# Another order of the first loads, sums of absolutes on ACT for the first weights, and scratch rows of 1 KB, in a chunked-attention and mixture-of-experts kernel

## The chip, the cores and the metric

One core of a Trainium2 chip runs the whole program in one launch. The engines are PE (matrix products and transposes), ACT (activations, copies with a scale), DVE (elementwise work and reductions), POOL (elementwise work, slower) and SP, which here only issues DMAs. The metric is the device time of the program in us; less is better.

## The reference

Attention in chunks of 32 tokens, each with 16 tokens of context to its left, 8 to its right and 8 memory tokens; then eight experts on all tokens, their outputs weighted by a matrix P that eight rounds of row and column scaling make out of gate logits.

```python
def _attn_ref(q, k, v, mem_k, mem_v):      # q, k, v: (4, 8, 768, 64), mem: (4, 8, 8, 64)
    for c in range(nc):                    # 24 chunks of 32
        k_full = np.concatenate([mem_k, k[:, :, l_start:r_end]], axis=2)
        v_full = np.concatenate([mem_v, v[:, :, l_start:r_end]], axis=2)
        scores = scale * np.matmul(q_c, k_full.transpose(0, 1, 3, 2))
        a = np.exp(scores - np.max(scores, axis=-1, keepdims=True))
        a = a / (np.sum(a, axis=-1, keepdims=True) + 1e-09)
        out[:, :, c_start:c_end] = np.matmul(a, v_full)

def _moe_ref(x, w_gate, w1, w2):           # x: (3072, 512), w1: (8, 512, 1024), w2: (8, 1024, 512)
    logits = x @ w_gate
    P = np.exp(logits - logits.max())
    for _ in range(8):
        P /= P.sum(1, keepdims=True) + 1e-09
        P /= P.sum(0, keepdims=True) + 1e-09
        P *= N / E
    for e in range(E):
        out += P[:, e:e + 1] * (np.maximum(x @ w1[e], 0.0) @ w2[e])
```

## The kernel before

**Work.** The 3072 tokens are 24 blocks of 128 for the attention (6 per batch) and 6 units of 512 for the experts, so four blocks feed one unit. There are 48 pairs of expert and unit. Products of the experts run in float16, each operand split in a high and a low half (`split`: ACT writes the high half, DVE the rest), three matmuls for one; and by Strassen's scheme of seven products instead of eight (`px`, `py`, `pz` for x times w1, `yx`, `yy`, `yz` for h times w2). Expert 0 in its first unit goes without that scheme (`pp` for x times w1, `yp` for h times w2), since it needs less preparation. The first of these `pp` products is called the first product below.

**Scales.** Before a matrix is split it is scaled by a power of two. For weights, `most` takes the largest absolute value of each partition of a staged tile on DVE (`mxs`), `scales` reduces over the four tiles (`most_of`), PE transposes that column (`row_w`), DVE reduces it, and PE spreads the result to all partitions (`sp_w`); the scale `sw` follows. For the tokens, the values v give the bound (`vmax`, `row_x`, `sp_x`, `sx`).

**Attention of a block.** q and k are loaded by SP (`load_block`), a few rows of the neighbour and the memory keys as `kx` (`load_extra`), values as windows of 56 rows (`load_values`, tiles `v_pair`, `w_0_2`, `w_0_3`, `x_room`). PE transposes q, k and kx (`tq`, `tk`, `tx`), ACT copies them (`qT`, `kC`, `kxT`), PE makes scores (`sp`), DVE the softmax's maximum and difference, ACT the exponential (`s`), PE transposes (`ta`), ACT copies (`at`), PE multiplies by the values (`xp`), DVE divides (`xq`), PE transposes (`xt`) and ACT copies into `xg`, the unit's tokens.

**Order.** A planner (`Plan`) holds all tasks with a cost, an engine and a due time, runs them through in a model of its own, and so writes the order of every engine once, when the program is built; on the chip each engine works through its row in order and waits on semaphores. DMAs have a cost in that model too (`dma=`, `ISSUE`, `BEHIND`, `FIRST`). Where the model sees a gap on PE of over 0.4 us, `pad` fills it with matmuls on the identity that nobody reads (`warm`), so that PE stays busy. Their number is fixed in the program.

**Scratch.** Tokens in their split form are kept in DRAM (`xkeep`, 1.8 MB a unit) and loaded again for each expert; the sums of the outputs (`akeep`) and some tokens (`gkeep`) as well. A tile of w1 is two loads of 256 KB with rows of 512 bytes.

Of the kernel before, what the change touches and what calls it, by code (L numbers as in the profile page):

```python
# [11 lines left out]
F16 = mybir.dt.float16  # L12
# [9 lines left out]
SHIFT = 11  # L22
HSHIFT = 18
ISSUE = 0.5
BEHIND = 5.0
FIRST = 2.0
MARGIN = 8.0
APART = 3.6
# [3 lines left out]
class Task:  # L32


    __slots__ = ("eng", "cost", "fn", "prio", "left", "ready", "end", "then", "takes", "frees", "n", "dma", "start", "many")
# [55 lines left out]
class Plan:  # L91
# [14 lines left out]
    def add(self, eng, cost, fn, deps=(), prio=0.0, bufs=(), takes=None, frees=None, dma=0.0, many=False):  # L106
# [3 lines left out]
        t.many = many  # L110
        if dma:
            t.cost = cost * ISSUE
# [51 lines left out]
    def run(self):  # L164
        clock = {e: 0.0 for e in self.ENGINES}
        waiting = {e: [] for e in self.ENGINES}
        able = {e: [] for e in self.ENGINES}
        dma = FIRST
# [4 lines left out]
        while left:  # L173
# [45 lines left out]
            for s in t.then:  # L219
                s.left -= 1  # L220
                late = lag
                if s.eng == t.eng and not t.dma:
                    late = 0.0
                elif t.dma and self.fill is not None:

                    late = MARGIN if s.prio - t.end > FAR else 0.0
# [7 lines left out]
def tile_chunked_attn_sinkhorn_moe(  # L234
# [83 lines left out]
    ones = one.broadcast_to([P, P])  # L318
    idle = ident.bitcast(BF16)
# [114 lines left out]
    def scales(part, s, u, name, deps, prio, pool=None):  # L434
# [20 lines left out]
        def inverse(a):  # L455
            nc.vector.tensor_scalar_mul(u, a, 2.0**-SHIFT)
# [74 lines left out]
    w1v = w1.rearrange("e (kt p) (fh fp f) -> e fp p kt fh f", p=P, fh=2, fp=FP)  # L531
    w2v = w2.rearrange("e (fh fp p) d -> e fp p fh d", fh=2, fp=FP)
# [3 lines left out]
    def load(e, fp, which, prio, ahead="", eng="SP", after=()):  # L536
        shape = [P, 2, KT, P] if which == 1 else [P, 2, DM]
# [8 lines left out]
        def go():  # L546
            if which == 1:
                for fh in range(2):
                    queue.dma_start(st.t[:, fh], w1v[e, fp, :, :, fh])
# [3 lines left out]
        return st, add(eng, 2 if which == 1 else 1, go, after, prio, [st], dma=2.1)  # L553

    def most(e, fp, which, st, deps, prio):
        def go():
            flat = st.t.rearrange("p a k f -> p (a k f)" if which == 1 else "p a d -> p (a d)")
# [10 lines left out]
    def scale_w(e, which, deps, prio, pool=None):  # L568
# [9 lines left out]
            pool,  # L578
        )
# [14 lines left out]
    def cut(e, fp, which, st, ld, prio):  # L594
# [12 lines left out]
        if which == 1:  # L607
            a11, a12 = lambda: st.t[:, 0, 0:2], lambda: st.t[:, 0, 2:4]
            a21, a22 = lambda: st.t[:, 1, 0:2], lambda: st.t[:, 1, 2:4]
# [25 lines left out]
        if which == 1:  # L635
# [3 lines left out]
                    lambda: st.t[:, 0],  # L639
# [21 lines left out]
        else:  # L661
            pieces = [(slice(2, 3), slice(0, 1), (0.5, 0.65)), (slice(4, 7), slice(1, 4), (0.9, 1.1))]
            deps = deps + o.users
        for to, of, costs in pieces:
            done.append(
                split(
                    lambda j, to=to: o.t[:, j, to].rearrange(flat),
                    lambda of=of: ws.t[:, of].rearrange(flat),
# [19 lines left out]
    def plain1(fp, st, ld, prio):  # L688

        o = operands("w1", [P, 2, 7, 2, P], f"w1_0_{fp}")  # L690
        done = split(
            lambda j: o.t[:, j, 0:4].rearrange("p o k f -> p (o k f)"),
            lambda: st.t.rearrange("p a k f -> p (a k f)"),
# [9 lines left out]
    def block1(e, i):  # L703
        return i if e > 0 else (0, 1, 3, 2, 4, 5, 6)[i]
# [22 lines left out]
    vfound = []  # L727
    sxs = {}
# [3 lines left out]
    BLOCKS = (-50.0, -44.0, -30.0, -26.0)  # L732
# [30 lines left out]
    def load_extra(u):  # L763
# [10 lines left out]
        for n in range(n0, n0 + BU):  # L774
# [5 lines left out]
            def go(b=b, blk=blk, r0=r0, t0=t0):  # L780
# [5 lines left out]
                elif blk == NB - 1:  # L786
                    nc.sync.dma_start(kx.t[r0 : r0 + LC], rows(k, b, S - LC, LC))
                    nc.sync.dma_start(kx.t[r0 + LC : r0 + KR], rows(k, b, 0, KR - LC))
                else:
# [5 lines left out]
                    2 if blk in (0, NB - 1) else 1,  # L795
# [1532 lines left out]
```

## Time and profile before

| what | value |
|---|---|
| median of 3 runs | 1921.61 us (1919.76 to 1923.17) |
| the profiled execution | 1919.81 us |
| its span, first to last instruction | 1917.9 us |
| PE busy | 1903.2 us, 99% |
| DVE busy | 1436.4 us, 75% |
| ACT busy | 1033.6 us, 54% |
| granted clock of PE | 1.00 |

The page is of one execution. A row of a timeline gives start, length, engine, line, operation, the tile written and those read, how many, and in brackets the idle time before it with what ended it. A row of the waits gives the engine and line that waited, what for, the sum in us, the number and the longest. PEld is the load of weights into PE, which runs beside PE.

### The profile page before, as it was taken

What the parts mean: (1) busy time and instruction counts of PE and PEld (TensorE: products, weight loads), DVE (VectorE), ACT (ScalarE), POOL (GpSimd) and SP (SyncE); (2) the same over time, 40 slices, a digit from 0 to 9 for tenths busy, and PEclk for the clock granted to TensorE, in tenths of its full rate; (3) what the DMA queues carried; (4) which work ended last, traced back from release to release, by engine and by line L of the source; (5) the groups of instructions that cost most, each with busy time, mean ns of one, the idle gap of its engine ahead of it and who ended that gap; (6) DMA issues with size and microseconds to landing.
All of it is one profiled execution on the core that took longest, in us unless ns stands there. A gap on an engine that the chain in (4) does not pass through costs nothing.

```text
span 1917.9 us, 47295 instructions
## 1 busy us (share of the span) xinstructions
PE 1903.2 (99%) x19616; PEld 1641.0 (86%) x19616; DVE 1436.4 (75%) x2396; ACT 1033.6 (54%) x2019; POOL 524.4 (27%) x549
## 2 busy tenths in 40 slices
PE   9999999999999999999999999999999999999999
PEld 7777676688888888888888888888888888888888
DVE  6776569778679866898668875898678885786565
ACT  4765565556456545646445554655555554564453
POOL 1220001544224221432124231342124232332112
PEclk9999999999999999999999999999999999999999
DMA  8678753453235342265214533245313732322321
GB/s 198 174 194 209 171 172 116 129 204 125 83 110 172 127 148 85 78 197 185 92 63 149 197 105 127 78 160 176 138 45 105 242 122 94 100 83 84 127 83 67
DMA packets 246791, 254.82 MB, mean 133 GB/s; under 512 B 113264, under 2 KB 180272, under 8 KB 242224
## 3 DMA queue, kind: packets, MB, share of 16 engines
q1 hardware_dynamic: 244452, 251.21, 41.2%
q8 instruction: 153, 2.51, 0.6%
q10 hardware_dynamic: 2124, 0.59, 0.2%
q14 instruction: 62, 0.51, 0.1%
HBM read 187.84 MB, written 63.44 MB: 131 GB/s over the span
## 4 chain that ended last, share of the span: by engine, by line
PE 96%; DMA 2%; DVE 1%; ACT 0%; issue 0%; SPq 0%; ACTq 0%; DVEq 0%
PE px L1598 26%; PE yx L1598 23%; PE pz L1598 13%; PE yz L1598 11%; PE py L1598 6%; PE yp L2126 6%; PE yy L1598 6%; DMA q<-in_q_dram 1%; PE xp L1137 1%; PE sp L1069 1%; PE pp L2045 1%; PE tq L1006 1%; PE tk L1010 0%; PE ta L1127 0%; PE xt L1178 0%; DVE w L521 0%
## 5 line engine op out<-in xcount | busy, mean ns | idle before, releaser
L1598 PEld LDWEIGHTS <-w 128*128 128x128 f16 x7896 | 771.4, 98 | 91.9 <-issue 0.6
L1598 PEld LDWEIGHTS <-h 128*128 128x128 f16 x7056 | 690.4, 98 | 81.4 <-issue 1.5
L1598 PE MATMUL px<-x,w 128*128 128x256 f16 x4512 | 549.1, 273 | 0.0
L1931 POOL TENSOR_TENSOR acc<-acc,y 128x256 f32<-128x256 f32 x252 | 267.5, 1068 | 862.1 <-ACT y L1906 842.7
L1598 PE MATMUL yx<-w,h 128*128 128x256 f16 x4032 | 467.5, 273 | 1.3 <-DVE acc L1941 1.3
L1657 ACT ACTIVATE q<-px 128x256 f32<-128x256 f32 x376 | 142.8, 381 | 294.2 <-PE px L1598 289.5
L1598 PE MATMUL pz<-x,w 128*128 128x256 f16 x2256 | 278.2, 273 | 0.0
L1598 PE MATMUL yz<-w,h 128*128 128x256 f16 x2016 | 233.8, 273 | 0.0
L1826 DVE TENSOR_TENSOR h<-ss,h 128x1024 f16<-128x1024 f32 x160 | 215.0, 1346 | 4.0 <-ACT h L1802 3.5
L1777 ACT ACTIVATE h<-c 128x768 f16<-128x768 f32 x168 | 140.8, 838 | 106.4 <-DVE c L1667 106.4
L1802 ACT CAST h<-ss 128x1024 f16<-128x1024 f32 x168 | 174.1, 1039 | 20.4 <-DVE ss L1766 19.6
L1766 DVE SCALAR_TENSOR_TENSOR ss<-c,ss 128x256 f32<-128x256 f32 x336 | 168.3, 501 | 8.2
L1810 DVE SCALAR_TENSOR_TENSOR h<-c,h 128x768 f16<-128x768 f32 x168 | 165.3, 984 | 9.2 <-ACT h L1777 9.1
L1667 DVE SCALAR_TENSOR_TENSOR c<-px,q 128x256 f32<-128x256 f32 x188 | 78.0, 422 | 103.2 <-PE px L1598 94.9
L1906 ACT ACTIVATE y<-yx,pscale 128x256 f32<-128x256 f32 x168 | 79.4, 473 | 114.8 <-PE yx L1598 110.6
L1598 PE MATMUL py<-x,w 128*128 128x256 f16 x1128 | 139.2, 273 | 0.0
L2126 PE MATMUL yp<-w,h 128*128 128x512 f16 x576 | 132.0, 379 | 0.0
L1667 DVE SCALAR_TENSOR_TENSOR c<-py,q 128x256 f32<-128x256 f32 x188 | 78.5, 422 | 60.2 <-PE py L1598 56.7
L1766 DVE SCALAR_TENSOR_TENSOR ss<-c,h 128x512 f32<-128x512 f32 x168 | 120.8, 719 | 3.1 <-ACT h L1754 3.0
L1598 PE MATMUL yy<-w,h 128*128 128x256 f16 x1008 | 116.9, 273 | 0.0
L2126 PEld LDWEIGHTS <-h 128*128 128x128 f16 x576 | 56.0, 98 | 57.9
L513 ACT ACTIVATE w<-ws,sw 128x1024 f16<-128x1024 f32 (+1 forms) x64 | 69.3, 1089 | 65.5 <-POOL ws L602 65.5
(158 smaller groups left out, 1773.0 us busy)
## 6 DMA issues: line engine op xcount, KB each, us to landing
x<-xkeep SPq DMA_DIRECT2D x28, 1792.0 KB
akeep<-acc SPq DMA_DIRECT2D x168, 256.0 KB
acc<-akeep SPq DMA_DIRECT2D x168, 256.0 KB
w1f<-in_moe_w_dram SPq DMA_DIRECT2D x72, 256.0 KB
w2f<-in_moe_w_dram SPq DMA_DIRECT2D x32, 512.0 KB
w1fm<-in_moe_w_dram SPq DMA_DIRECT2D x56, 256.0 KB
w2fm<-in_moe_w_dram SPq DMA_DIRECT2D x28, 512.0 KB
xkeep<-x SPq DMA_DIRECT2D x6, 1792.0 KB
```

Of the source, the lines that this page charges most:

```text
L513: lambda: nc.scalar.activation(dst(0), src(), AF.Copy, scale=s),
L1598: nc.tensor.matmul(dst.t, a, b, start=(not more and n == 0), stop=(n == end), skip_group_check=more,)
L1657: lambda: nc.scalar.activation(t.t, src.t, AF.Copy, scale=DOWN),
L1667: lambda: nc.vector.scalar_tensor_tensor(c.t[:, o], src.t, DOWN, q.t, op0=ALU.mult, op1=ALU.add),
L1766: lambda: nc.vector.scalar_tensor_tensor(dst(), src(), 0.0, other(), op0=ALU.max, op1=op),
L1777: lambda: nc.scalar.activation(h.t[:, 0, 0:3], c.t, AF.Relu),
L1802: lambda: nc.scalar.copy(h.t[:, 0, 3:7], ss.t),
L1810: lambda: nc.vector.scalar_tensor_tensor(h.t[:, 1, 0:3].rearrange("p a n -> p (a n)"), c.t.rearrange("p a n -> p (a n)"), 0.0, h.t[:, 0, 0 ...
L1826: lambda: spare.tensor_tensor(h.t[:, 1, 3:7], ss.t, h.t[:, 0, 3:7], op=ALU.subtract),
L1906: (lambda: nc.scalar.activation(t.t, src.t, AF.Copy, scale=f))
L1931: lambda: nc.gpsimd.tensor_tensor(acc.t[:, cols], acc.t[:, cols], q.t, op=ALU.add),
L2126: nc.tensor.matmul(py.t, hf.t[:, hl, where[fh], o : o + P], room(fp, WIDE * wl + DM * fh, WIDE * wl + DM * (fh + 1)), start=(fp == 0 and i ...
```

## The change

It has four parts. **First loads:** SP now issues q, k and kx of blocks 0 and 1 ahead of all values; the values of those two blocks come as 2 + 8 larger loads, all by SP, where SP and ACT shared them; some rows that only masked places see are not loaded any more (two small pieces of k and v per batch end), and zeros are written for block 0 by POOL. ACT does an exponential of one column at the start, which brings the table load to the front. **First weights:** a tile of w1 is one load with rows of 1 KB (the columns of the two halves are neighbours now, and the tiles are addressed accordingly), and the four w1 and four w2 tiles of expert 0 get their bound from a sum of absolutes on ACT (`total`) where DVE took maxima; their scale has a shift of 13 for 11. **Scratch:** `xkeep`, `gkeep` and `akeep` have rows of 1 KB in DRAM, where they had 14 KB, 4 KB and 2 KB. **Planner:** other constants, DMA costs and due times, and a model of eight loads in flight.

```diff
-ISSUE = 0.5
-BEHIND = 5.0
-FIRST = 2.0
+ISSUE = 0.45
+LANES = 8
+BEFORE = 0.7
+TABLE = 2.2
...
-APART = 3.6
+APART = 2.5
...
-                at = max(at, dma - BEHIND)
-                t.start = at
-                clock[t.eng] = at + t.cost
-                dma = max(dma, at + t.cost / 2) + t.dma
-                t.end = max(dma, at + t.cost) + 2.6
+                t.start = max(at, lanes[0])
+                for _ in range(t.count):
+                    at = max(at, lanes.pop(0))
+                    dma = max(dma, at + BEGIN) + t.dma / t.count
+                    lanes.append(dma + AFTER)
+                    at += ISSUE
+                clock[t.eng] = at
+                t.end = dma + AFTER
...
+    first = misc.tile([P, 1], F32, name="first")
+    nc.scalar.activation(first, one, AF.Exp)
...
-    xkeep = [dram.tile([P, 2 * 7 * 2 * GT], F16, name=f"xkeep_{u}") for u in range(NU)]
-    gkeep = [dram.tile([P, KT * GT], F32, name=f"gkeep_{g}") for g in range(2 * NU)]
-    akeep = [dram.tile([P, DM], F32, name=f"akeep_{T}") for T in range(NT)]
+    xkeep = [dram.tile([2 * 7, P, 2 * GT], F16, name=f"xkeep_{u}") for u in range(NU)]
+    gkeep = [dram.tile([KT, P, GT], F32, name=f"gkeep_{g}") for g in range(2 * NU)]
+    akeep = [dram.tile([2, P, DH], F32, name=f"akeep_{T}") for T in range(NT)]
...
-    w1v = w1.rearrange("e (kt p) (fh fp f) -> e fp p kt fh f", p=P, fh=2, fp=FP)
-    w2v = w2.rearrange("e (fh fp p) d -> e fp p fh d", fh=2, fp=FP)
+    w1v = w1.rearrange("e (kt p) (fp f) -> e fp p kt f", p=P, fp=FP)
+    w2v = w2.rearrange("e (fp fh p) d -> e fp p fh d", fh=2, fp=FP)
...
-                for fh in range(2):
-                    queue.dma_start(st.t[:, fh], w1v[e, fp, :, :, fh])
+                queue.dma_start(st.t.rearrange("p k a f -> p k (a f)"), w1v[e, fp])
...
+    def total(e, fp, which, st, deps, prio):
+        def go():
+            nc.scalar.activation(
+                room(0, 0, 1024),
+                st.t.rearrange("p k a f -> p (k a f)" if which == 1 else "p a d -> p (a d)"),
+                AF.Abs,
+                accum_out=mxs[:, e, which - 1, fp : fp + 1],
+            )
+
+        return add("ACT", 1.2, go, deps, prio, [st, first2[0]])
...
-    BLOCKS = (-50.0, -44.0, -30.0, -26.0)
+    BLOCKS = (-50.0, -49.0, -30.0, -26.0)
...
+        if n == 0:
+            ks.append(add("POOL", 0.2, lambda: nc.gpsimd.memset(kt.t[0:LC], 0.0), (), at, [kt]))
...
+            if n == 0:
+                lv = [
+                    add("SP", 2 + 2 * HP, lambda: go_both(nc.sync), (), at, [vt], dma=4.2),
+                    add("POOL", 0.2, clear, (), at, [vt]),
+                ]
+            elif n == 1:
+                lv = list(vs[0][1])
...
-            at = START - 14.0 + n // 2 * 17.0
-            vfound.append(add("DVE", 1.21, most, lv, at, [vt]))
-            if n == BU // 2 - 1:
-                scale_x(NU, vmax[:, 0:2], vfound, START - 12.0)
+            at = (5.0, 12.0, 33.0, 33.0)[n]
...
-            found.append(most(0, fp, which, st, [ld], at - 12.0))
-        scale_w(0, which, found, at - 10.0, "att")
+            found.append(total(0, fp, which, st, [ld], at - 12.0))
+        scale_w(0, which, found, at - 10.0, "att", SHIFT + 2)
```

What the planner makes of it shows in the rows of the engines (line, operation, tile written, tiles read, shape). On SP, the issue of the first loads, before, up to the first weights (`w1f`); nine more loads of `v_pair` stood in ACT's row:

```order
L848 DMA q_165<-in_q_dram 128x8x64
L842 DMA k_167<-in_k_dram 16x8x64
L843 DMA k_167<-in_k_dram 112x8x64
L782 DMA kx_175<-in_k_dram 24x8x64
L783 DMA kx_175<-in_mem_k_dram 8x8x64
L790 DMA kx_175<-in_k_dram 32x8x64
L921 DMA v_pair<-in_v_dram 16x4x64
L921 DMA v_pair<-in_v_dram 40x4x64
L921 DMA v_pair<-in_v_dram 56x4x64 x3
L848 DMA q_188<-in_q_dram 128x8x64
L845 DMA k_192<-in_k_dram 128x8x64
L790 DMA kx_175<-in_k_dram 32x8x64 x2
```

On SP after the change, the same place:

```order
L880 DMA q_165<-in_q_dram 128x8x64
L875 DMA k_163<-in_k_dram 112x8x64
L816 DMA kx_172<-in_k_dram 24x8x64
L817 DMA kx_172<-in_mem_k_dram 8x8x64
L823 DMA kx_172<-in_k_dram 32x8x64
L880 DMA q_178<-in_q_dram 128x8x64
L877 DMA k_180<-in_k_dram 128x8x64
L823 DMA kx_172<-in_k_dram 32x8x64 x2
L959 DMA v_pair<-in_v_dram 40x4x64 x2
L967 DMA v_pair<-in_v_dram 56x7x64 x8
L943 DMA v_pair<-v_pair 8x7x260 x2
L560 DMA w1f_0_325<-in_moe_w_dram 128x4x256
```

The second block's q and k moved ahead of the values, and the weights follow the values as one load a tile. On DVE, before, from the maxima of the first weights to the first row that splits them (`w_0_0`):

```order
L558 TENSOR_REDUCE mxs<-w1f_3_376 128x1
L502 TENSOR_REDUCE most_of<-row_x_564 1x1
L450 TENSOR_SCALAR most_of<-most_of 1x1
L451 TENSOR_SCALAR most_of<-most_of 1x1
L445 TENSOR_REDUCE most_of<-mxs 128x1
L456 TENSOR_SCALAR ux<-sp_x_617 128x1
```

On ACT after the change, where the sums of the first weights stand (they write `mxs`; the tile `w_0_0` takes the absolutes, which nobody reads):

```order
L581 ACTIVATE w_0_0_434,mxs<-w1f_0_325 128x1024
L1171 ACTIVATE s_436<-s_436 128x512
L581 ACTIVATE w_0_0_434,mxs<-w1f_1_327 128x1024
L1247 COPY xg_476<-xt_465 128x4x128
L1209 COPY at_481<-ta_471 128x512
L581 ACTIVATE w_0_0_434,mxs<-w1f_2_330 128x1024
L581 ACTIVATE w_0_0_434,mxs<-w1f_3_332 128x1024
```

The four passes over the weights left DVE's row and stand in ACT's, between the copies of the attention. In DVE's row the reduction of the third block's values (`vmax<-w_0_2`) also moved, from ahead of the first weight's split to behind the fourth. On SP at the first store of tokens to `xkeep`, before:

```order
L2150 DMA akeep_134<-acc_0_1398 128x512
L549 DMA w1f_1_1423<-in_moe_w_dram 128x4x128 x2
L1256 DMA xkeep_116<-x_626 128x7168
L848 DMA q_1463<-in_q_dram 128x8x64
L845 DMA k_1564<-in_k_dram 128x8x64
L790 DMA kx_1589<-in_k_dram 32x8x64 x3
```

and after:

```order
L877 DMA k_1323<-in_k_dram 128x8x64
L823 DMA kx_1332<-in_k_dram 32x8x64 x3
L821 DMA kx_1332<-in_k_dram 16x8x64
L560 DMA w1f_2_1354<-in_moe_w_dram 128x4x256
L2219 DMA akeep_136<-acc_0_1350 128x2x256
L925 DMA v_pair<-in_mem_v_dram 8x4x64 x2
L1319 DMA xkeep_118<-x_575 128x14x512
L975 DMA v_pair<-in_v_dram 56x4x64 x8
```

Here q and k of a block stood behind the store, and values stand behind it now. PE's row holds the same products in both; the filling matmuls fall from 168 to 106, those ahead of the first product from 157 to 106.

More of the change, by code (lines that the diff above doesn't have):

```diff
@@ L23 @@
 HSHIFT = 18
-ISSUE = 0.5
-BEHIND = 5.0
-FIRST = 2.0
+ISSUE = 0.45
+LANES = 8
+BEFORE = 0.7
+TABLE = 2.2
+BEGIN = 1.0
+AFTER = 1.2
+LATER = 1.0
 MARGIN = 8.0
-APART = 3.6
+APART = 2.5
 FAR = 60.0
 class Task:
-    __slots__ = ("eng", "cost", "fn", "prio", "left", "ready", "end", "then", "takes", "frees", "n", "dma", "start", "many")
+    __slots__ = ("eng", "cost", "fn", "prio", "left", "ready", "end", "then", "takes", "frees", "n", "dma", "start", "many", "count")
 class Past:
@@ L110, in add @@
         t.many = many
+        t.count = cost
         if dma:
@@ L164, in run @@
     def run(self):
-        clock = {e: 0.0 for e in self.ENGINES}
+        clock = dict.fromkeys(self.ENGINES, BEFORE)
+        clock["ACT"] = TABLE
         waiting = {e: [] for e in self.ENGINES}
         able = {e: [] for e in self.ENGINES}
-        dma = FIRST
+        dma = 0.0
+        lanes = [0.0] * LANES
         for t in self.tasks:
@@ L224, in run @@
                 elif t.dma and self.fill is not None:
-                    late = MARGIN if s.prio - t.end > FAR else 0.0
+                    late = MARGIN if s.prio - t.end > FAR else LATER if s.eng == "PE" else 0.0
                 s.ready = max(s.ready, t.end + late)
@@ L536, in load @@
     def load(e, fp, which, prio, ahead="", eng="SP", after=()):
-        shape = [P, 2, KT, P] if which == 1 else [P, 2, DM]
+        shape = [P, KT, 2, P] if which == 1 else [P, 2, DM]
         place = "stage", stage
@@ L727, in tile_chunked_attn_sinkhorn_moe @@
     vfound = []
+    second = []
     sxs = {}
@@ L794, in load_extra @@
                     "SP",
[L795 removed]
+                    2 if blk == 0 else 1,
                     go,
@@ L1106, in scores @@
         )
+        if n == 1:
+            found, lv, vt = second.pop()
+            vfound.append(add("DVE", 1.21, found, [t, *lv], 12.0, [vt]))
+            scale_x(NU, vmax[:, 0:2], list(vfound), 13.0)
         t = add(
```

149 lines of the change are left out of this document (94 added, 55 removed).

## The prediction

> **What bounds the kernel now.** I read the page first, then the waits of PE, then PE's busy time by stretch, then the timeline of the stretch that stood out. The first fence holds the page's line of busy times, three rows of the stretches (us, then busy time of PE, PEld, DVE, ACT, POOL, granted clock, share of DMA, GB/s) and the waits of PE after its first product.
>
> ```profile
> PE 1903.2 (99%) x19616; PEld 1641.0 (86%) x19616; DVE 1436.4 (75%) x2396; ACT 1033.6 (54%) x2019; POOL 524.4 (27%) x549
> ...
> 36.00:200.00 164.00, 157.81 (x2888) 118.65 (x2887) 116.57 (x208) 103.71 (x211) 25.43 (x32) 1.00 0.77 195
> 200.00:1000.00 800.00, 798.59 (x7811) 676.68 (x7810) 610.37 (x1036) 443.61 (x861) 237.03 (x236) 1.00 0.41 132
> 1000.00:1918.00 918.00, 914.72 (x8380) 819.61 (x8377) 690.06 (x1118) 470.00 (x919) 257.04 (x270) 1.00 0.35 120
> ...
> PE xp L1137 <- issue: 2.5, 2, 1.7
> PE tq L1006 <- DMA q<-in_q_dram: 2.4, 3, 1.1
> PE yx L1598 <- DVE acc L1941: 1.3, 1, 1.3
> PE xp L1137 <- DVE lg L1430: 0.9, 1, 0.9
> PE tk L1010 <- PE xp L1137: 0.2, 1, 0.2
> ```
>
> PE is the bound, at a granted clock of 1.00. From 200 us on it idles for 1.4 us in 800 and for 3.3 us in 918, the latter mostly the end, where the last output leaves. All waits behind the first product sum to 7.3 us. So the time is the moment of the first product, plus a fixed amount of matmul work, plus these waits. The timelines of PE, DVE and ACT over the start show that moment and what precedes it (start, length, engine, line):
>
> ```profile
> 1.56 6.54 PE L427 MATMUL warm<-ident 128*128 128x256 bf16 x44 [1.56 <-POOL ident masks.py:199]
> ...
> 29.57 0.38 PE L481 MATMUL sp_w<-most_of,one 1*128 1x1 f32 x2
> 29.88 3.67 PE L427 MATMUL warm<-ident 128*128 128x256 bf16 x32
> 33.38 1.14 PE L2045 MATMUL pp<-x,w 128*128 128x256 f16 x6
> ...
> 9.14 1.28 ACT L1034 ACT_TABLE_LOAD   x1 [9.14 <-DMA v_pair<-in_v_dram]
> 10.44 0.60 ACT L1034 ACTIVATE qT<-tq 128x512 f32<-128x512 f32 x1
> ...
> 21.72 2.34 DVE L558 TENSOR_REDUCE mxs<-w1f 128x1 f32<-128x1024 f32 x2
> 24.12 1.22 DVE L558 TENSOR_REDUCE mxs<-w1f 128x1 f32<-128x1024 f32 x1
> ...
> 26.36 1.21 DVE L558 TENSOR_REDUCE mxs<-w1f 128x1 f32<-128x1024 f32 x1
> ...
> 28.04 0.13 DVE L445 TENSOR_REDUCE most_of<-mxs 128x1 f32<-128x4 f32 x1
> ...
> 31.44 1.22 DVE L974 TENSOR_REDUCE vmax<-w 128x1 f32<-128x1024 f32 x1
> ```
>
> The first product starts at 33.38. Before it stand the attention of two blocks and 157 matmuls of filling (warm), whose number the planner fixed when the program was built. Two things hold the start: ACT issues its loads and then its table load before the first copy at 10.44, and DVE does the four maxima of the first weights until 27.57, the scale after them, and then, at 31.44, a reduction of the third block's values ahead of its split of the weights.
>
> **Term A, the first product.** The orders of the two kernels hold the same 180 matmuls of real work ahead of the first product; the filling there falls from 157 to 106 (31, 4, 12, 8, 12, 3, 7 and 29). A filling matmul takes 3.50/32 = 0.109 us from start to start. At the very start they are slower: 18 begin by 5.0 us. So the filling and the work leave the floor: the 31 first ones end at about 5.0 + 13 x 0.11 = 6.4 instead of 7.95 (-1.5), and the other 75 instead of 113 take 4.1 less. That gives -5.6 if every wait stays; with all waits of that stretch (2.0 us) gone too, -7.6. No filling can go below that, so -7.6 is one end.
>
> The other limit is when the data are there. These are the stretches of the start and SP's issue of the weights:
>
> ```profile
> 0.00:5.00 5.00, 3.44 (x18) 2.50 (x18) 0.14 (x2) 0.00 (x0) 0.91 (x8) 1.00 0.55 123
> 5.00:10.00 5.00, 5.00 (x48) 4.58 (x46) 0.00 (x0) 0.86 (x1) 0.00 (x0) 1.00 0.66 117
> 10.00:15.00 5.00, 4.78 (x101) 3.87 (x100) 1.34 (x3) 2.82 (x8) 1.82 (x2) 1.00 0.96 193
> 15.00:20.00 5.00, 4.03 (x149) 3.15 (x147) 3.04 (x6) 3.13 (x7) 2.22 (x3) 1.00 0.87 206
> 20.00:25.00 5.00, 4.55 (x98) 3.63 (x96) 4.97 (x7) 1.80 (x3) 0.00 (x0) 1.00 1.08 302
> ...
> SPq L782 <- DMA q<-in_q_dram: 1.8, 1, 1.8
> ...
> 15.94 5.81 SPq L549 DMA_DIRECT2D w1f<-in_moe_w_dram  x8
> ```
>
> In the first 10 us the DMA engines are busy for 0.6 of the time, since many small loads (16 rows of k, 8 of mem_k) hold places for which the next load must wait: SP's fourth load waited 1.8 us for q. The new order puts nine loads first, all but one of 48 to 256 KB. Ahead of the first weights stand q and k of two blocks, kx, and values: 256 + 224 + 256 + 512 + 864 + 130 KB = 2.30 MB; then 2.10 MB of weights. If the engines are full from 2 us on, 2.30 MB at 193 to 206 GB/s take 11.5 us and 2.10 MB at 302 take 6.9: the last weights land at 20.4. At the old rates (3.20 MB by 20 us and 302 GB/s from there) 4.40 MB would be there at 24.0. I take 21.5, nearer the full engines, since large loads now stand first. ACT then sums the last tile: the nearest rows are a cast and a scaled copy of the same shape.
>
> ```profile
> L1802 ACT CAST h<-ss 128x1024 f16<-128x1024 f32 x168 | 174.1, 1039 | 20.4 <-DVE ss L1766 19.6
> L513 ACT ACTIVATE w<-ws,sw 128x1024 f16<-128x1024 f32 (+1 forms) x64 | 69.3, 1089 | 65.5 <-POOL ws L602 65.5
> ```
>
> That is 1.1 us with a bound of 2.2 if an accumulating pass ran at half the rate, which no row shows. From the reduction of the maxima (28.04) to sp_w (29.57) the chain takes 1.5; from sp_w to the product 3.8 with 32 filling matmuls, 3.5 with 29. So the product starts at 21.5 + 1.1 + 0.2 + 1.5 + 3.5 = 27.8, by the bounds of the landing at 26.7 to 30.3. The split of the weights by DVE (1.28 each) now stands ahead of the reduction of the third block's values, so no load holds it. A = 27.8 - 33.4 = **-5.6**, ends -7.6 and -2.0 (the late landing and the slow pass together); a loss is excluded unless the weights land after 27.1. The two paths agree, which is why I trust it.
>
> Inside A at no cost: eight passes of 1.1 us move from DVE to ACT; in 15 to 25 us ACT is busy for 4.9 of 10. Between the first loads ACT also copies for the attention, and each sum stands in its in-order queue: a late tile holds the copies behind it, which is in the end of 30.3. The nine loads that ACT issued go to SP, 25 issues of 0.45 = 11 us ahead of the last weights, less than the 21.5 of the data. The two copies of mem_v on SP wait for a load that ACT issues after its table load; SP reaches them at its 20th issue, 9 us at the earliest, so nothing waits. POOL's three small memsets fall to an engine that is busy for 27% of the span.
>
> **Term B, filling after the first product.** The order loses 3 + 6 + 2 = 11 such matmuls: **-1.2**. Ends -1.2 and 0, if PE would wait there anyway.
>
> **Term C, waits for q.** The chain of waits shows that q takes 10.05 and 8.84 us where it is issued right behind a store of 1.8 MB, and PE waits for it.
>
> ```profile
> 78.32 0.60 SPq L1256 DMA_DIRECT2D xkeep<-x  x1
> ...
> xkeep<-x SPq DMA_DIRECT2D x6, 1792.0 KB
> ...
> 79.01 10.05 DMA q<-in_q_dram
> ...
> 169.15 8.84 DMA q<-in_q_dram
> ...
> 89.10 0.66 PE L1006 MATMUL tq<-ident,q 128*128 128x128 f32 x4 [1.10 <-DMA q<-in_q_dram]
> 103.42 0.63 PE L1006 MATMUL tq<-ident,q 128*128 128x128 f32 x4 [0.35 <-DMA q<-in_q_dram]
> 178.03 0.66 PE L1006 MATMUL tq<-ident,q 128*128 128x128 f32 x4 [1.00 <-DMA q<-in_q_dram]
> 131.80 0.35 PE L1137 MATMUL xp<-v_pair,at 64*32 64x65 f32 x16 [1.68 <-issue]
> ```
>
> In the new order two pairs of q and k stand ahead of the first store, and values come behind it. C = **-2.4**, ends -4.3 (the 1.68 and 0.2 at 131 us, which also follow a store, go too) and 0. What is late next are those values. [...]
>
> The scratch in rows of 1 KB costs nothing else: behind 200 us only 1.3 us of PE's waits hang on it (yx on acc). No wait for x is among them; a load of x, as large as the store, would take 9.5 us even at the 193 GB/s of 256-byte rows.
>
> **Term D, new waits.** ACT now sums the second weights (4 x 1.1) in front of copies that free PSUM, where DVE's maxima stood before. The second of them stands behind 2.47 MB after the first weights; at 193 to 302 GB/s it lands at 30 to 34. ACT gets there some 6 us behind the first product (an estimate: 36 matmuls of 0.11 and the attention's pieces between them), at 34. With values behind the store I put **+1.5** for D, one wait of the size seen (1.1) and a half; ends 0 and +4.
>
> **Sum.** -5.6 - 1.2 - 2.4 + 1.5 = -7.7. The profiled execution took 1919.81 (span 1917.9 and 1.9 around it): 1912.1. The median shown is 1.8 higher, 1921.61, so 1913.9 on its scale.
>
> **Rivals.**
> (1) The data come late and the waits stay: A -3.1, B and C 0, D +1.5, so -1.6 to -4: 1917.6 to 1920. For it: the first 10 us of DMA at 120 GB/s. Against: the small loads that caused them are gone.
> (2) All goes: A -7.6, B -1.2, C -4.3, D 0: 1908.5. Against: PE's own filling is cut to a plan that has some waits in it.
> (3) The other side: ACT blocked by the second weights. Every us that the third or fourth lands after about 36 stops the copies that free PSUM, and PE one for one. It takes back the gain at 44 and is slower by over 0.2% from 48. Against: the fourth stands 1.05 MB behind the second, 5.4 us at 193 GB/s, so 40 at the latest by these rates, which is the end of D.
> (4) PE cools: of the filling matmuls 6 to 7 begin in a us before 4.5 us, 11 after 5.5.
>
> ```profile
> 3.50:4.50 1.00, 1.00 (x6) 0.72 (x5) 1.00 0.66 150
> ...
> 5.50:6.50 1.00, 1.00 (x11) 0.90 (x10) 1.00 1.01 161
> ```
>
> [...] The longest rest in the start of this trace was 0.57, too short to tell. [...]
>
> **How the numbers follow.** My forecast 0.60, rival (1) 0.17, (2) 0.13, (3) 0.05, (4) 0.05. The predicted time is 1914; the range 1909 to 1919 takes in (2) but for its end, the forecast, (4) and half of (1). About 0.2%, 3.8 us, is what a measurement tells from no change: below 1917.8 lie the forecast, (2), (4) and a third of (1), 0.84; within 0.2% 0.11; slower 0.05.
>
> **What would show it.** The first product at 26.7 to 30.3; 106 filling matmuls, none after it; the table load in the first 3 us; eight sums on ACT near 1.1 us; no wait of PE for q over 0.4; PE's waits after the first product 3 to 7 us; no change beyond 200 us. I am wrong if the product starts early and the sum of waits behind it grows by as much, or if the last first weights land after 25.

## The result and the profile after

The changed kernel is slower: 1944.50 us median (1942.80 to 1950.62) against 1921.61, a ratio of 1.0127 with a 95% interval of 1.0114 to 1.0139. I had forecast 1914, range 1909 to 1919. The profiled execution took 1945.22, its span is 1943.4, so 25.5 more than before.

The first fence holds the page's line of busy times after the change and three rows of the stretches (us, then busy time of PE, PEld, DVE, ACT, POOL, granted clock, share of DMA, GB/s).

```profile
PE 1906.5 (98%) x19554; PEld 1637.2 (84%) x19554; DVE 1418.6 (73%) x2388; ACT 1038.1 (53%) x2036; POOL 525.0 (27%) x552
...
36.00:200.00 164.00, 156.45 (x2860) 116.63 (x2858) 109.55 (x211) 104.54 (x215) 24.35 (x32) 0.99 0.77 192
200.00:1000.00 800.00, 785.41 (x7644) 661.24 (x7642) 588.97 (x1002) 428.32 (x836) 229.32 (x230) 1.00 0.43 132
1000.00:1918.00 918.00, 911.62 (x8340) 815.29 (x8338) 697.78 (x1132) 479.52 (x938) 260.95 (x269) 1.00 0.37 117
```

The matmuls are 62 fewer, all of them filling, and yet PE is busy for 3.3 us more and idle for 36.9 us where it was 14.7. The new idle time is not at the start: between 200 and 1000 us PE idled for 1.4 before and idles for 14.6 now. The waits (engine and line, what for, sum in us, number, longest) say what for:

```profile
DVE mxs L569 <- DMA w1fm<-in_moe_w_dram: 30.1, 13, 4.3
ACT acc L1926 <- DMA acc<-akeep: 18.4, 13, 3.8
PE px L1664 <- DVE c L1733: 14.1, 12, 2.3
DVE mxs L569 <- DMA w2fm<-in_moe_w_dram: 9.4, 6, 2.9
DVE xt L1356 <- DMA xs<-gkeep: 7.4, 2, 6.7
PE tq L1065 <- DMA q<-in_q_dram: 4.9, 3, 3.6
PE ta L1190 <- ACT s L1171: 3.9, 1, 3.9
PE px L1664 <- ACT q L1723: 3.4, 4, 1.4
```

Read from the DVE rows: DVE reaches the maxima of the later experts' weights (`w1fm`, `w2fm`) 19 times before the tile has landed, 39.5 us in all; before it was 5 times and 5.0. The drain (`c`, L1733) of a PSUM bank stands behind the waiting reduction in DVE's row, and PE waits for that drain 12 times, 14.1 us, a wait that the trace of before does not list. ACT does the same with the sums of the outputs (18.4, before 5.4). PE's waits behind the first product sum to 28.6 us, before 7.3.

One case, in the chain of waits (start, length, what) and then in the timelines of DVE and PE:

```profile
36.76 7.76 DMA q<-in_q_dram
...
250.50 4.21 DMA xs<-gkeep
...
1060.09 4.35 DMA w2fm<-in_moe_w_dram
1066.82 7.12 DMA w1fm<-in_moe_w_dram
```

```profile
1070.52 1.15 DVE L1876 SCALAR_TENSOR_TENSOR h<-c,h 128x768 f16<-128x768 f32 x1
1073.96 1.22 DVE L569 TENSOR_REDUCE mxs<-w1fm 128x1 f32<-128x1024 f32 x1 [2.30 <-DMA w1fm<-in_moe_w_dram]
...
1080.82 1.47 PE L1664 MATMUL px<-x,w 128*128 128x256 f16 x12 [2.31 <-DVE c L1733]
```

The tile is issued at 1066.82 and lands 7.12 us later; the reduction is the next thing in DVE's row after 1071.7, waits 2.30, and 7 us on PE waits 2.31 for DVE. The same pair comes back about every 222 us, once an expert. The planner's model explains why the reduction stands there. For a lone tile of w1 it now reckons 1.0 + 1.45 + 1.2 = 3.65 us from issue to landing; the model of before reckoned 0.5 + 2.1 + 2.6 = 5.2. For a block of sums it is 2.9 where it was 4.15. Tiles of `w1fm` took 6.07 to 7.12 in this chain, `w2fm` 4.31 to 4.92.

The second loss is the clock. Stretches of 2 us of PE (busy time, granted clock, DMA share, GB/s):

```profile
46.00:48.00 2.00, 2.00 (x69) 0.50 0.32 67
...
260.00:262.00 2.00, 2.00 (x10) 0.50 0.00 0
...
858.00:860.00 2.00, 2.00 (x12) 0.50 0.02 6
```

Behind PE's waits of 3.60 (until 44.66, for q), 3.94 (until 259.00) and 2.09 us (until 856.28) the clock is halved for 3.41 us each. Three times half of 3.41 is 5.1 us.

So of the 25.5 us: waits behind the first product +21.3, clock +5.1, first product -2.8 (30.57 for 33.38), 11 fewer filling matmuls behind it -1.2. That is 22.4. The other 3 us are no waits: from the first product to the end PE idles for 32.1 us where it was 10.9, which is the same rise once more, and is busy for 1880.7 where it was 1873.6, +7.1, of which clock and filling explain 3.9. By an estimate they are the edges of the waits: 12 matmuls in a row last 1.47 us, but the next 12 begin 1.31 us after the first of them (1074.41, 1075.72), so each wait costs some 0.16 us more than its row says, and there are 28 waits where there were 8, so 3.2 us.

### The profile page after: what moved, and what is told of

Read it like the earlier page. It is cut to its first block, busy times and chain, and to the rows that moved or that the text cites. A ratio compares the mean times of both kernels' runs of the same rounds, so it can differ in the third digit from the quotient of the medians.

```text
span 1943.4 us, 47052 instructions
## 1 busy us (share of the span) xinstructions
PE 1906.5 (98%) x19554; PEld 1637.2 (84%) x19554; DVE 1418.6 (73%) x2388; ACT 1038.1 (53%) x2036; POOL 525.0 (27%) x552
## 4 chain that ended last, share of the span: by engine, by line
PE 87%; DMA 6%; DVE 5%; issue 1%; ACT 1%; SPq 0%; POOL 0%; DVEq 0%; ACTq 0%; POOLq 0%
PE px L1664 22%; PE yx L1664 22%; PE pz L1664 11%; PE yz L1664 11%; PE yy L1664 6%; PE yp L2195 6%; PE py L1664 5%; DMA w1fm<-in_moe_w_dram 2%; DVE ss L1832 1%; PE xp L1200 1%; DMA w2fm<-in_moe_w_dram 1%; DVE w L533 1%; DMA acc<-akeep 1%; PE pp L2114 1%; DMA akeep<-acc 1%
## 5 line engine op out<-in xcount | busy, mean ns | idle before, releaser
L1664 PE MATMUL px<-x,w 128*128 128x256 f16 x4512 | 550.0, 273 | 17.6 <-DVE c L1733 14.1
L1892 DVE TENSOR_TENSOR h<-ss,h 128x1024 f16<-128x1024 f32 x160 | 210.4, 1316 | 5.5 <-ACT h L1868 5.5
L1868 ACT CAST h<-ss 128x1024 f16<-128x1024 f32 x168 | 174.7, 1040 | 45.7 <-DVE ss L1832 45.2
L1733 DVE SCALAR_TENSOR_TENSOR c<-px,q 128x256 f32<-128x256 f32 x188 | 76.7, 421 | 105.5 <-PE px L1664 85.7
L1733 DVE SCALAR_TENSOR_TENSOR c<-py,q 128x256 f32<-128x256 f32 x188 | 78.4, 422 | 61.8 <-PE py L1664 52.4
```

The source lines that it names most:

```text
L1664: nc.tensor.matmul(dst.t, a, b, start=(not more and n == 0), stop=(n == end), skip_group_check=more,)
L1733: lambda: nc.vector.scalar_tensor_tensor(c.t[:, o], src.t, DOWN, q.t, op0=ALU.mult, op1=ALU.add),
L1868: lambda: nc.scalar.copy(h.t[:, 0, 3:7], ss.t),
L1892: lambda: spare.tensor_tensor(h.t[:, 1, 3:7], ss.t, h.t[:, 0, 3:7], op=ALU.subtract),
```

## The experiments

My theory, M: the planner's new DMA model alone, with nothing else of the change, sets the readers of loads too early in the in-order rows. Rivals: R, rows of 1 KB make the transfers slower, so that loads are late; S, the new start shifts everything behind it. Each ratio below is against the kernel before on the same chip, with its 95% interval; idle is span less PE's busy time of the profiled execution. The last three columns are of that one execution, which can lie off the median: for "changed, landing 1.4 later" it took 1923.55.

| kernel | us | ratio | first product | PE idle | clock |
|---|---|---|---|---|---|
| before | 1921.61 | 1 | 33.38 | 14.7 | 1.000 |
| changed | 1944.50 | 1.0127 [1.0114, 1.0139] | 30.57 | 36.9 | 0.997 |
| before, scratch rows of 1 KB | 1920.21 | 1.0004 [0.9995, 1.0014] | 33.89 | 14.4 | 1.000 |
| changed, scratch rows of before | 1938.72 | 1.0099 [1.0083, 1.0114] | 30.77 | 31.5 | 0.998 |
| changed, DMA model and costs of before | 1918.34 | 0.9991 [0.9981, 1.0001] | 32.46 | 12.6 | 1.000 |
| before, new DMA model and costs | 1945.23 | 1.0127 [1.0111, 1.0142] | 38.21 | 36.0 | 0.996 |
| changed, landing 1.4 later | 1919.02 | 0.9992 [0.9982, 1.0002] | 30.82 | 19.5 | 0.998 |
| changed, costs of before | 1921.88 | 1.0000 [0.9991, 1.0010] | 30.87 | 15.6 | 0.999 |
| changed, landing 3 later behind 36 us | 1921.28 | 0.9999 [0.9989, 1.0008] | 30.71 | 18.7 | 0.998 |
| changed, landing and costs later behind 36 us | 1925.43 | 1.0022 [1.0013, 1.0032] | 31.24 | 20.8 | 0.996 |
| changed, copies in `v_pair` 2.2 later | 1946.37 | 1.0129 [1.0114, 1.0144] | 35.15 | 33.5 | 0.996 |
| landing 1.4 later, PE's readers 3 more | 1927.73 | 1.0037 [1.0026, 1.0048] | 30.45 | 22.6 | 0.999 |
| landing 1.4 later, second weights behind q | 1920.53 | 0.9999 [0.9990, 1.0009] | 30.00 | 18.7 | 0.999 |
| changed, landing and costs later throughout | 1921.62 | 1.0004 [0.9993, 1.0015] | 30.89 | 15.1 | 0.999 |

### One part alone, one part undone

**The rows of the scratch alone**, put into the kernel before:

```diff
-    xkeep = [dram.tile([P, 2 * 7 * 2 * GT], F16, name=f"xkeep_{u}") for u in range(NU)]
+    xkeep = [dram.tile([2 * 7, P, 2 * GT], F16, name=f"xkeep_{u}") for u in range(NU)]
     # gkeep and akeep likewise
```

> The kernel before with one part of the change: the scratch in DRAM in rows of 1 KB; planner, costs and order of every engine as before. Theory M (the planner's new DMA model puts the readers of loads too early in the in-order rows of DVE and ACT, so they hold PE): within 3 us of the time before, 1919 to 1925, and DVE waits for w1fm and w2fm about 5 us as before. Theory R (rows of 1 KB make the scratch traffic, or what shares the queue with it, slower): at least half of the loss of 23 us, 1933 or more. Theory S (the new start shifts DVE and ACT work that is then missing later): as M.

1920.21, ratio 1.0004 [0.9995, 1.0014]: the rows cost nothing that can be measured in this order. R is out as the cause of the loss. The load of q behind the first store did not get later either: PE's waits for q sum to 2.4 us in three waits, as before.

**The changed kernel without the rows**, planned as changed:

```diff
-    xkeep = [dram.tile([2 * 7, P, 2 * GT], F16, name=f"xkeep_{u}") for u in range(NU)]
+    xkeep = [dram.tile([P, 2 * 7 * 2 * GT], F16, name=f"xkeep_{u}") for u in range(NU)]
```

> The changed kernel without the part on the scratch: rows of 14, 4 and 2 KB again, the planner's costs left as changed, so every engine's order stays. Theory M: no help, 1940 to 1950, DVE waits for w1fm still over 25 us. Theory R: back by at least half, below 1933. Theory S: as M.

```profile
DVE mxs L569 <- DMA w1fm<-in_moe_w_dram: 24.6, 13, 3.7
...
PE px L1661 <- DVE c L1730: 10.1, 13, 1.8
```

1938.72: most of the loss stays, with the same waits, on the whole a little shorter; theory M's figures (1940 to 1950, over 25 us) were just missed. Whether the 0.3% between this kernel and the changed one belongs to the rows (once the plan has no slack left) isn't settled: the two were not timed side by side, and their intervals touch.

**The DMA model of before in the changed kernel**, with its costs (2.1 for a tile of weights, 1.3 for a block of sums, 7.0 for a unit of tokens):

```diff
-                t.start = max(at, lanes[0])
-                for _ in range(t.count):
-                    at = max(at, lanes.pop(0))
-                    dma = max(dma, at + BEGIN) + t.dma / t.count
-                    lanes.append(dma + AFTER)
-                    at += ISSUE
-                clock[t.eng] = at
-                t.end = dma + AFTER
+                at = max(at, dma - BEHIND)
+                t.start = at
+                clock[t.eng] = at + t.cost
+                dma = max(dma, at + t.cost / 2) + t.dma
+                t.end = max(dma, at + t.cost) + 2.6
```

> The changed kernel with the planner's DMA model and DMA costs of before (loads, order at the start, sums on ACT and rows of 1 KB stay as changed). Theory M: the loss goes, 1914 to 1925; DVE's waits for w1fm and w2fm fall from 39 us to under 10 and PE's waits behind the first product from 28 us to under 10. Theory R and theory S: 1938 or more.

The waits, and the stretches:

```profile
DVE mxs L563 <- DMA w2fm<-in_moe_w_dram: 1.3, 2, 0.8
DVE mxs L563 <- DMA w1fm<-in_moe_w_dram: 0.5, 1, 0.5
...
PE px L1658 <- DVE c L1727: 0.5, 1, 0.5
```

```profile
36.00:200.00 164.00, 160.66 (x2964) 120.52 (x2962) 113.25 (x218) 109.82 (x225) 25.17 (x32) 1.00 0.77 192
200.00:1000.00 800.00, 797.31 (x7749) 675.99 (x7748) 612.62 (x1024) 439.74 (x851) 238.77 (x238) 1.00 0.42 132
```

1918.34: DVE's waits fall from 39.5 to 1.8 us and the whole loss is gone, with the new first loads, the sums on ACT and the rows all in place. Behind the first product no PE wait beyond 1.23 us is left and no spell at half the clock. What remains of the change is worth about 0.1%; the interval runs from a gain of 0.2% to none.

**The new DMA model in the kernel before** is the same edit the other way round.

> The kernel before with only the planner's new DMA model and DMA costs (start, maxima on DVE and rows as before). Theory M: slower by 10 to 25 us, 1932 to 1947, with DVE waiting over 20 us for w1fm and w2fm. Theory R and theory S: 1918 to 1925.

```profile
DVE mxs L567 <- DMA w1fm<-in_moe_w_dram: 30.4, 12, 8.0
DVE mxs L567 <- DMA w2fm<-in_moe_w_dram: 8.3, 6, 2.9
```

1945.23, a ratio of 1.0127: a loss as large as that of the whole change, out of this one part. That the two ratios agree to the last digit is luck: here the first product also comes 4.8 us later than before (38.21), PE's waits behind it sum to 23.7 us for 28.6 in the changed kernel, and there are four spells at half the clock for three. S is out: the loss is here without the new first loads, and it was gone with them. So M is shown from both sides, for the planner's new constants as a whole: the two edits also exchange `APART` and `LATER`, which are not loads' costs. The next two kernels keep these as changed.

### Which number of the model

```diff
 # landing 1.4 later
-                t.end = dma + AFTER
+                t.end = dma + 2.6
```

> The changed kernel, but the planner takes a load to have landed 2.6 us behind its bytes, where the change says 1.2; its DMA costs stay as changed. Which part of the planner's model is at fault? Theory L (the landing): a load of 512 KB took 6.07 us from issue to landing where the changed plan says 3.65; with 1.4 us more most readers in DVE's and ACT's rows stand behind their loads, the waits of DVE for the weights fall from 33 us to under 12, the waits of PE behind the first product from 28 to under 14, and the time is 1920 to 1928. Theory C (the costs of the bytes, 1.45 and 0.7 where 2.1 and 1.3 stood): the landing alone leaves DVE's waits over 25 us and the time over 1936.

```diff
 # costs of before, landing as changed
-        return st, add(eng, 1, go, after, prio, [st], dma=1.45 if which == 1 else 1.35)
+        return st, add(eng, 1, go, after, prio, [st], dma=2.1)
 # and the sums 1.3 for 0.7, the tokens 7.0 for 4.3, q and k 1.55 for 1.2, values by the same ratio
```

> The changed kernel with the DMA costs of the kernel before (2.1 for a weight tile, 7.0 for a unit of tokens, 1.3 for a block's sums) and the landing of 1.2 as changed. Theory L: a lone load is planned only 0.65 us later, DVE's 13 waits for the first weight tiles shrink by about that each, 30 to some 20 us, and the time is 1932 to 1940. Theory C: the waits go, DVE's under 10 us, and the time is 1918 to 1926.

The waits of the first and of the second:

```profile
DVE mxs L569 <- DMA w1fm<-in_moe_w_dram: 5.8, 5, 1.8
PE tq L1065 <- DMA q<-in_q_dram: 2.8, 1, 2.8
```

```profile
DVE mxs L569 <- DMA w2fm<-in_moe_w_dram: 9.2, 7, 1.6
PE pp L2114 <- issue: 3.0, 1, 3.0
DVE mxs L569 <- DMA w1fm<-in_moe_w_dram: 2.8, 2, 1.6
```

1919.02 and 1921.88: either mends nearly all, with `APART` and `LATER` as changed, so it is the time that the planner gives a load, and neither theory L (the landing alone) nor C (the costs alone) is right as I put it. I had reckoned with a lone load in the second; my reading, not tested, is that loads follow one another, and where a unit of tokens is charged 2.7 us more, every load behind it is planned later by as much. DVE still waits for 12.0 us in the second, and yet PE waits for `c` only 0.7: how much of DVE's waiting reaches PE is not a fixed share. In the first, PE's wait for q, at 45.7, is followed by 6.83 us at half the clock, twice the 3.4 that I reckon with below.

### Keeping the early first product

Both of these start at 30.8 and end no earlier than the kernel with the old model, which starts at 32.46. I tried four plans to keep that start.

```diff
 # landing 3 later for loads issued behind 36 us of the plan
-                t.end = dma + AFTER
+                t.end = dma + (AFTER if at < 36.0 else 4.2)
```

> The changed kernel, with the planner's landing at 4.2 us behind the bytes for every load issued later than 36 us of the plan; the start is planned as changed. Theory L: no reader comes too early; DVE's waits for weights under 3 us, none of ACT for sums, no half-clock spell but perhaps the one at 44 us, PE's waits behind the first product under 10 us; first product at 30.6 to 31.4 as in the changed kernel: 1915 to 1918. Rival S (the waits come from the new start, which leaves the row of loads in a worse order): waits stay, over 1935. Rival O (landing set too late now delays readers so that other work of theirs comes late): PE waits on DVE for c or on ACT, 1920 to 1930.

```diff
 # costs 1.5 times and landing 2.6, behind 36 us of the plan
-                    dma = max(dma, at + BEGIN) + t.dma / t.count
+                    dma = max(dma, at + BEGIN) + t.dma * (1.0 if at < 36.0 else 1.5) / t.count
-                t.end = dma + AFTER
+                t.end = dma + (AFTER if at < 36.0 else 2.6)
```

> The changed kernel, with the start planned as changed and, for loads issued later than 36 us of the plan, a landing of 2.6 us and costs of the bytes 1.5 times as high, which is about the model of the kernel before. Theory L or C: both parts are mended, DVE's waits for weights under 3 us, PE's behind the first product under 9 us, and the time 1914.5 to 1917.5, the best of all so far, since the first product stays 1.5 us ahead of that of the changed kernel with the old model throughout. Rival S: over 1935.

```diff
 # landing 2.6; the readers on PE of later loads 4 us on, where LATER is 1
-                    late = MARGIN if s.prio - t.end > FAR else LATER if s.eng == "PE" else 0.0
+                    late = MARGIN if s.prio - t.end > FAR else (LATER if t.end < 30.0 else 4.0) if s.eng == "PE" else 0.0
```

> The planner takes a load to have landed 2.6 us behind its bytes (as in the kernel with the later landing, 1919.0), and for readers on PE of loads that end later than 30 us another 4 us (1 us before), so that PE is given other work or filling ahead of a transpose of q. Theory K (the clock): the wait of 2.8 us for q at 45.7 with the spell of 3.4 us at half the clock behind it goes, the granted clock is 1.000, 3 to 5 us: 1914 to 1917. Rival N: the readers of q then come late for the blocks behind them, new waits of the same size: 1918 to 1921.

```diff
 # landing 2.6; third and fourth tile of the second first weights behind q of the fifth block
-            st, ld = load(0, fp, which, FIRST[which - 1] + 0.5 * fp)
+            st, ld = load(0, fp, which, (FIRST[which - 1] if which == 1 or fp < 2 else 15.0) + 0.5 * fp)
```

> The planner with the landing of 2.6 us, and the third and fourth tile of the second first weights due behind q and k of the fifth block, which stood behind them. Theory K: q lands some 3 us earlier, the wait at 45.7 falls under 1 us and no spell at half the clock follows it: 1914 to 1917. Rival: the second weights are late instead, PE waits for their split (yp on DVE) at 50 to 60 us by 2 us or more: 1918 to 1921.

All four missed what I hoped for: 1921.28, 1925.43, 1927.73 and 1920.53. The waits that answer to it, one fence a kernel in that order:

```profile
PE tq L1065 <- DMA q<-in_q_dram: 5.9, 2, 3.1
```

```profile
PE sp L1128 <- issue: 3.2, 2, 2.4
PE tq L1065 <- DMA q<-in_q_dram: 3.1, 1, 3.1
```

```profile
DVE mxs L569 <- DMA w1fm<-in_moe_w_dram: 14.4, 9, 4.4
PE tq L1065 <- DMA q<-in_q_dram: 3.9, 1, 3.9
PE xp L1200 <- issue: 2.7, 1, 2.7
```

```profile
PE row_x L506 <- DVE most_of L457: 2.5, 2, 2.1
PE row_w L506 <- DVE most_of L457: 1.4, 1, 1.4
```

In the first two DVE waits for no weights any more, as expected, but the gain of the start goes back in the first 200 us: two waits of 2.4 to 3.1 us, each with a spell at half the clock. The second of them has one more spell, of 6.83 us from 18.24 on, ahead of its first product, behind two short waits for the copies in `v_pair` (1.41 and 0.54 us). In the third the wait for q moved from 45.7 to 99.6, and the plan that made room for it brought DVE's early reading back. In the fourth the wait for q did go and the first product came at 30.00, but the wait for the scale of the tokens, 1.5 us in the kernel with the later landing, grew to 2.1 with a spell behind it, and one of 1.4 for the scale of the second weights came; the rival's price was right and its place was not. The waits that read "issue" have no cause in the profile; a single one lasts up to 3.0 us in these kernels, and they stay open.

```diff
 # landing and costs both as before, the eight loads in flight as changed
-                t.end = dma + AFTER
+                t.end = dma + 2.6
```

> The changed kernel with both the costs of the kernel before and the landing of 2.6 us; only the eight loads in flight are left of the new model. Either alone brought the time back to 1919 to 1922. If what is left there is single waits in the first 200 us, both together give 1916 to 1920 with the waits of DVE for weights under 3 us, and filling after the first product keeps the clock at 1.000. Rival: the eight loads in flight are themselves at fault, and the time stays over 1921.

1921.62, DVE's waits for weights 0.5 us, PE idle 15.1, near the 14.7 of before. The expected 1920 was missed, and the time is over the 1921 that I had set as the rival's mark, but the rows do not bear the rival out: behind 202 us PE waits at most 0.35 us at a time, so the eight loads in flight do no harm there. In the first 200 us 4.7 us of waits with no seen cause, one of them followed by a spell, keep the time where it was.

### What held the first product

```diff
 # the two copies inside v_pair, and no other load, planned 2.2 us later
-                t.end = dma + AFTER
+                t.end = dma + AFTER + (2.2 if abs(t.prio + 46.9) < 0.01 else 0.0)
```

> The changed kernel, whose planner is told that the two copies inside v_pair land 2.2 us later than it assumed (they took 4.60 us from issue to landing where the plan had 2.4); all other loads are planned as changed. It tests what held the first product at 31.3. Theory V (the reduction of the first values stands in DVE's row ahead of the second block's softmax and waits 3.9 us for these copies): the softmax comes first, DVE's wait there falls under 1.5 us, PE's waits for DVE in the start go, and the first product comes at 29 to 30.5. Rival W (the first weights' sums on ACT are the limit in any case): 30.5 to 31.5. The waits beyond 200 us stay, so the time is 1938 to 1946 by both.

In the changed kernel DVE waits 3.89 us for these copies, ahead of the second block's softmax, and ACT's sums run as in the second fence:

```profile
17.35 1.22 DVE L1032 TENSOR_REDUCE vmax<-v_pair 128x1 f32<-128x1024 f32 x1 [3.89 <-DMA v_pair<-v_pair]
```

```profile
18.43 1.06 ACT L581 ACTIVATE w<-w1f 128x1024 f16<-128x1024 f32 x1 [2.45 <-DMA w1f<-in_moe_w_dram]
19.39 0.19 ACT L581 ACTIVATION_READ_ACCUMULATOR w<-w1f 128x1 f32 x1
...
23.90 1.06 ACT L581 ACTIVATE w<-w1f 128x1024 f16<-128x1024 f32 x1
24.86 0.19 ACT L581 ACTIVATION_READ_ACCUMULATOR w<-w1f 128x1 f32 x1
```

(The first product of the changed kernel came at 30.57, not at the 31.3 of the expectation.) With the copies planned later, in ACT's and PE's rows:

```profile
24.23 1.06 ACT L581 ACTIVATE w<-w1f 128x1024 f16<-128x1024 f32 x1 [1.53 <-DMA w1f<-in_moe_w_dram]
```

```profile
25.90 0.37 PE L506 MATMUL row_w<-ident,most_of 128*1 128x128 f32 x1 [3.05 <-ACT xg L1247]
```

The softmax did come first, and the last sum ended at 25.4, in the changed kernel at 25.05: here it waits for its tile until 24.2, and in the changed kernel the tile landed at 23.7 by the records of its semaphore, 0.2 us ahead of its sum. Theory V falls. W holds in so far as nothing ahead of these sums brought them forward, and what they wait for is the landing of the last first weights; its time, 30.5 to 31.5, was missed. The product came even later, at 35.15, and the kernel took 1946.37: with the softmax done earlier PE had nothing left ahead of `row_w`, waited 3.05 us for the sums and for the copy `xg` that stood behind them in ACT's row, and the clock was halved for 6.83 us behind that wait.

## Why the prediction was wrong

**Term D and "no change beyond 200 us" failed**, and with them the sum. I put +1.5 (ends 0 and +4) for new waits, all of them in the first 200 us; they came to +21.3, most of them behind 200 us, and the clock took 5.1 us more. It is the sign of being wrong that I had named: the product starts early, and the waits behind it grow by more. The step: I took the planner's new constants for a matter of the start, and read from the trace of before that only 1.3 us of PE's waits behind 200 us hang on the scratch. That row told how the *old order* stood to the loads. The order is written from the model, and the change cut the assumed landing of a tile of w1 from 5.2 to 3.65 us; the trace of before had landings to hold against such numbers, and I held none. For a load of q, 256 KB, the changed model reckons 1.0 + 1.2 + 1.2 = 3.4 us, and the chain of waits of before has 4.34, 8.84 and 10.05. The two kernels with the model exchanged show that this part alone makes such a loss (1.0127) and its absence removes it (0.9991).

**Term A** was the right mechanism in the wrong size: -2.8 for -5.6, inside its ends of -7.6 and -2.0, though the product at 30.57 is just past the 26.7 to 30.3 that I gave for it. The term mis-sized is the landing of the last first weights: 23.7 where I took 21.5. The old rates had given 24.0, and I preferred the full engines. From the end of the last sum the chain took 5.5 us, by my working 5.2. The sum on ACT took 1.06 and 0.19 for reading the accumulator (1.1 taken; the bound of 2.2 was not needed). The other path was misread too: I let the first 31 filling matmuls end at 6.4, and they ended at 7.8, since they began every 0.21 us until 7.2 us where in the trace of before this slow start ended at 4.9. What moved its end is not shown. That the two paths agreed, which is why I trusted the number, was thus chance. And the real work ahead of the first product is 310 matmuls in both traces, not 180; no sum used that number.

**Term B** held: 106 filling matmuls, none behind the first product. Whether the missing filling left waits bare that then cost the clock is not shown: the kernel with landing and costs later throughout has 23 filling matmuls behind the first product, and a spell all the same.

**Term C** had the wrong sign. Behind the first store the wait for q shrank to 0.86, but q of the fifth block is now issued behind the second weights and 16 loads of values and lands after 7.76 us, when PE has waited 3.60: waits for q 4.9 us where 2.4 stood. "What are late next are those values" named the wrong load.

**The scratch rows** at no cost: right in the order of before (1.0004); in the changed order some 0.3% stays open. **The table load** came at 0.72, as forecast.

**The rivals.** (4), PE cools, happened three times, though not in the thinner filling but behind waits: 3.41 us at half the clock each time, so 1.7 us lost. From 4.8 us to its end the trace of before has no such spell that could have priced it. That the clock column read 1.00 over the slow start of before tells nothing, since the records of the clock begin at 4.8 us there. The 6 to 7 and 11 matmuls in a us that I read there count some that began before the stretch; from start to start it is 0.213 and 0.109 us, about a half. (3) did not: ACT's sums of the second weights waited 1.6 us in all. That the planner's order elsewhere would get worse was none of my rivals, and the 0.05 for slower was far too little.

## What to carry to other kernels

Where a planner writes the order, an edit of its cost model is an edit of every stage: compare the new assumed times with measured landings from the trace before costing anything else, and price the in-order engine that reads too soon, not only PE. A plan that was too optimistic about loads was worse here than one that was too cautious: 1.4 us more of assumed landing was worth 1.3%, and 1.6 us more on top, for loads behind 36 us of the plan, cost nothing clear. A gain at the start counts only if the waits behind it are looked at as closely as the first product.

## What the runs showed of the hardware

The clock fell behind waits of PE of some 2 us and more. Over the 14 profiled executions, none of 20 PE waits of 1.5 to 1.9 us was followed by a spell at half the clock, 9 of 12 waits of 1.96 to 2.75 us were, and all 12 of 2.8 to 3.9. Of the 22 spells between the slow start and PE's last product, 18 lasted 3.41 us and so cost about 1.7, and 4 lasted 6.83.

In the trace of the changed kernel the spells show what tells its waits apart. They begin at 44.73, 259.77 and 857.10 us, that is 63 and 175 times 3.413 us, the length of a spell, from one to the next. Divide the trace, from 10 us on, into pieces of that length that start or end at these moments, and sum PE's idle time in each: the pieces ahead of the three spells have 3.34, 2.75 and 2.09 us, and up to 1939 us no other has more than 1.85 (1078.97 to 1082.38), with the clock at 1.00 behind it. So the wait of 2.09 us, which falls into one piece, cost the clock (from 857.10 on), and the longer one of 2.31 us, which is split between two, did not (stretch, its length, PE busy, granted clock, DMA share, GB/s):

```profile
853.69:857.10 3.41, 1.32 (x13) 1.00 0.98 326
...
1075.56:1078.97 3.41, 2.94 (x27) 1.00 1.09 348
1078.97:1082.39 3.42, 1.57 (x15) 1.00 0.69 237
```

For the other two waits of 1.96 to 2.75 us without a spell behind them (2.3 us at 255.8 in the changed kernel with the scratch rows of before, 2.7 at 132.2 in the one with PE's readers 3 more) it is not shown. Why four spells lasted twice as long is open.

The tiles of weights of 512 KB that stand in the chain of waits of the changed kernel, those that somebody waited for, took 4.3 to 7.1 us from issue to landing while other loads were in flight (between 1064 and 1080 us the DMA engines' share is 1.08, in the trace of before 0.16). The fourth tile of the first weights, issued at 15.28 behind the loads of the start, took 8.5. Rows of 1 KB in place of 2 to 14 KB made no difference to the time in the order of before (ratio 1.0004, with an interval of 0.9995 to 1.0014).
